# Where the matmul operands of a convolution and hard-swish kernel lie in SBUF: other offsets for w_in, y and y_other

## The chip, the cores and the metric

The kernel runs on one core of a Trainium2 chip. The time is the device time of one execution in microseconds (us), and the profile is one execution taken by the hardware profiler. Engines are named as in the profile: PE is TensorE's matmul, PEld its weight load, DVE is VectorE, ACT is ScalarE, POOL is GpSimd, SP is SyncE. SBUF is the on-chip memory of 128 partitions from which all of them read; an offset here is a byte address within a partition, the same in all partitions.

## What is computed

A depthwise causal convolution of 7 taps along the sequence, whose weights are a softmax per head, is followed by two dense layers with a hard-swish between them:

```
w   = exp(weight - max); w = w / (sum(w) + 1e-9)          # 8 heads x 7 taps
y   = sum over k of w[h, k] * x[b, s + k - 6, h, :]        # x: 8 x 4096 x 192
h   = y @ w_in                                            # 32768 x 192 @ 192 x 2048
g   = h * clip(h + 3, 0, 6) / 6
out = g @ w_out                                           # 2048 x 192
```

Everything is fp32 (the weights of the dense layers come as float64 words).

## The kernel before, in words

The 32768 tokens are worked on in 32 blocks of 1024. A block has two stages on TensorE.

First layer (`first_layer`, `products`, L443). A block of y is held as 128 partitions x 3 x 512: the lower 64 partitions have one half of the block's tokens, the upper 64 the other; the 192 channels are 64 partitions x 3. To keep fp32 accuracy with float32r matmuls, both operands are split: y into a high and a low part (`y_own`, tiles y0 and y1), w_in into a high, a low and a full part (`w_in_parts`, tiles w_in0, w_in1, w_in2). `PASSES` says which meet: (w_in0, y0), (w_in1, y0), (w_in2, y1). A unit of the first layer is 3 passes x 3 channel groups x 2 partition halves = 18 matmuls of 64x512, that is nine pairs; the two of a pair use the two halves of the array's rows, the lower for 128 hidden channels of its tokens, the upper for another 128 of its own. Each matmul has a weight load of 64x128. 8 units read `y_own`; 8 more read `y_other`, the same numbers with the partition halves exchanged by DMA, which gives each half of the tokens the hidden channels that it still lacks (`swap`, L304 and L305). So a block has 288 matmuls at L443 in 144 pairs. ACT (`relu`, L316) and DVE (`gate`, L320) make g from each unit's two PSUM banks.

Second layer (`second_layer`, L583). It is a two-level Strassen-like scheme over g, sums of g and sums of w_out. Four column groups of 32 run side by side, in an order that is written out by hand: each matmul has a due time in units of a 256-column matmul, and the list is sorted by these. Operands that move are g, the sums S1 and S3 (tiles s1 and s3), z, z_other and z_early; weights are w_out, w_s and w_s4. The sums S3 are made behind the gates of the first layer's second half by POOL (`g_sums`, L390) and, for the last chunks, by DVE; POOL makes the small sums too (`small_sums`, L541) and issues accumulating DMAs (L486, L775, L980). One of the second layer's streams begins with products of S3. The convolution of the block after the next (L966, L969) runs on ACT and DVE beside all this; `split_high`, `split_rest` and `swap_parts` then make the next block's operands.

The first block is different: before it the weights are rounded from float64 words, chunk by chunk, in `Rounding` (L192 to L232; L229, L230 and L231 write the three parts of w_in), between the units.

Tiles are placed in the order in which they are asked for, pool after pool (cst, xs, ys, yo, ot, and then the pools of the start or of the rest), each rounded up to 32 bytes. Worked out from the sizes, offsets before, relative to a multiple of 64:

| tiles | offset |
|---|---|
| g, w_in0, w_in1, w_in2, w_out, w_s, w_s4 | 32 |
| y0, y1 (also z_early), y_other (also z_other) | 32 |
| y (unsplit), results, s1, s3, z, p1, p4 | 0 |

Within these tiles all matmul operands start at multiples of 128 bytes.

Two tiles of the softmax are touched: `mx` (the maximum, in pool ot at L117) and `sm` (the sum, in pool yo at L126), one word each per partition; `e_sb` (the exponentials, L264) has a tile of its own. They are used at L263 to L268 and at L872 to L877, once, at the start.

Of the kernel before, what the change touches and what calls it, by code (L numbers as in the profile page):

```python
# [8 lines left out]
ALU = mybir.AluOpType  # L9
ACT = mybir.ActivationFunctionType  # L10
AX = mybir.AxisListType
F32 = mybir.dt.float32
# [19 lines left out]
def kernel(  # L32
# [8 lines left out]
    nc = tc.nc  # L41
    P = nc.NUM_PARTITIONS

    B, D, S = xT.shape
    H, KC = weight.shape
# [7 lines left out]
    K3 = D // D2  # L53
# [7 lines left out]
    NP = NC // 2  # L61
# [5 lines left out]
    cst = ctx.enter_context(tc.tile_pool(name="cst", bufs=1))  # L67
    xs = ctx.enter_context(tc.tile_pool(name="xs", bufs=1))
    ys = ctx.enter_context(tc.tile_pool(name="ys", bufs=1))
    yo = ctx.enter_context(tc.tile_pool(name="yo", bufs=1))  # L70
    ot = ctx.enter_context(tc.tile_pool(name="ot", bufs=1))
# [21 lines left out]
    w_sb = cst.tile([P, KC], F32, name="w_sb")  # L93
    for base, dma in ((0, nc.scalar), (D2, nc.sync)):
        dma.dma_start(
            out=w_sb[base : base + D2],
            in_=weight.unsqueeze(1).to_broadcast([H, GJ, KC]),
# [16 lines left out]
    make_identity(nc, ident[:])  # L114
    diag = cnv.tile([P, KC, P], F32, name="diag", bufs=1)
    g = cst.tile([P, NP, 2, G, N], F32, name="g")
    mx = ot.tile([P, 1], F32, name="mx")  # L117
    zeros = g[:, 0, 0, 0]
    nc.vector.memset(zeros, 0.0)


    w_in_parts = [cst.tile([P, NP, K3, P], F32, name=f"w_in{n}") for n in range(3)]
    def own_tiles(name):
        return [yo.tile([P, K3, N], F32, name=f"{name}{n}", tag=f"y{n}") for n in range(2)]

    sm = yo.tile([P, 1], F32, name="sm")  # L126
    y_own, z_early = own_tiles("y"), []

    def other_tile():
        return yo.tile([P, 2, K3, N], F32, name="y_other", tag="other")  # L130
# [127 lines left out]
    for n in range(5):  # L258
# [2 lines left out]
            load_x0(1, nc.sync, nc.sync)  # L261

    nc.vector.tensor_reduce(out=mx[:], in_=w_sb[:], axis=AX.X, op=ALU.max)  # L263
    e_sb = cst.tile([P, KC], F32, name="e_sb")  # L264
    nc.vector.tensor_tensor(
        out=e_sb[:], in0=w_sb[:], in1=mx[:].to_broadcast([P, KC]), op=ALU.subtract
    )
    nc.scalar.activation(e_sb[:], e_sb[:], ACT.Exp)  # L268

    c_sb = cst.tile([P, KC], F32, name="c_sb")  # L270
    half = cst.tile([P, 1], F32, name="half")
# [597 lines left out]
        units[n].part()  # L869

    with tc.manual_schedule():
        nc.vector.tensor_reduce(out=sm[:], in_=e_sb[:], axis=AX.X, op=ALU.add)  # L872
        nc.vector.tensor_scalar_add(sm[:], sm[:], 1e-9)
        nc.vector.reciprocal(sm[:], sm[:])
        nc.vector.tensor_tensor(
            out=c_sb[:], in0=e_sb[:], in1=sm[:].to_broadcast([P, KC]), op=ALU.mult
        )  # L877


# [12 lines left out]
        for _ in range(3):  # L892

            nc.tensor.matmul(  # L894
                out=psum[:, b], lhsT=zeros[:, 0:P], rhs=zeros, start=True, stop=True
# [92 lines left out]
        for r in range(2 * NP):  # L988
# [12 lines left out]
            n = joins.get(r)  # L1001
# [127 lines left out]
```

## Time and profile before

| | |
|---|---|
| median of 3 runs | 2198.15 us (2197.32 to 2198.38) |
| the profiled execution | 2197.43 us |
| its span, first to last instruction | 2195.7 us |
| granted TensorE clock | 0.999 |
| L443, first layer | 47% of the chain that ended last |
| L583, second layer | 49% |
| L443 matmuls, median ns of one | 386 |
| L443 weight loads, median ns | 184 |
| from one full block's start to the next | 67.47 us, of which the second layer 34.93 |
| first block | 17.3 to 94.7 us |

[...] The timeline of the profile gives the start of a group, its length, the engine, the line, what is written and read, and how many instructions are merged.

### The profile page before, as it was taken

What the parts mean: (1) busy time and instruction counts of PE and PEld (TensorE: products, weight loads), DVE (VectorE), ACT (ScalarE), POOL (GpSimd) and SP (SyncE); (2) the same over time, 40 slices, a digit from 0 to 9 for tenths busy, and PEclk for the clock granted to TensorE, in tenths of its full rate; (3) what the DMA queues carried; (4) which work ended last, traced back from release to release, by engine and by line L of the source; (5) the groups of instructions that cost most, each with busy time, mean ns of one, the idle gap of its engine ahead of it and who ended that gap; (6) DMA issues with size and microseconds to landing.
All of it is one profiled execution on the core that took longest, in us unless ns stands there. A gap on an engine that the chain in (4) does not pass through costs nothing.

```text
span 2195.7 us, 53684 instructions
## 1 busy us (share of the span) xinstructions
PE 2186.6 (100%) x23086; PEld 1568.1 (71%) x23086; DVE 1973.7 (90%) x1872; ACT 1267.6 (58%) x1761; POOL 1016.9 (46%) x864
## 2 busy tenths in 40 slices
PE   9999999999999999999999999999999999999998
PEld 5577776777777777777777767777777777677776
DVE  8889899899898998998988999989899998998987
ACT  7456565565655665555656556555566555565644
POOL 4545543355533555334554335553355533455433
PEclk9999999999999999999999999999999999999999
DMA  7366556756566665667555675656666566765564
GB/s 166 66 120 98 97 98 112 129 90 107 97 111 121 106 106 92 109 112 121 97 98 100 109 129 92 108 93 113 120 108 106 91 109 112 122 97 97 99 105 64
DMA packets 330557, 231.80 MB, mean 106 GB/s; under 512 B 209584, under 2 KB 294064, under 8 KB 330320
## 3 DMA queue, kind: packets, MB, share of 16 engines
q0 software_dynamic: 98688, 122.25, 36.5%
q1 hardware_dynamic: 230392, 105.86, 23.9%
q8 instruction: 181, 2.97, 0.6%
q14 instruction: 56, 0.46, 0.1%
q10 hardware_dynamic: 1240, 0.27, 0.1%
HBM read 31.72 MB, written 25.17 MB: 26 GB/s over the span
## 4 chain that ended last, share of the span: by engine, by line
PE 98%; DVE 1%; ACT 1%; POOL 0%; DMA 0%; issue 0%; DVEq 0%; ACTq 0%
PE psum L583 49%; PE psum L443 47%; PE psum L331 2%; PE psum L886 0%; PE psum L894 0%; DVE results L410 0%; ACT g L316 0%; DVE results L416 0%; DVE s L390 0%; DMA y_other<-y 0%; POOL w_in L231 0%; ACT scale L207 0%; ACT sig L204 0%; ACT sig L210 0%; POOL sig L221 0%
## 5 line engine op out<-in xcount | busy, mean ns | idle before, releaser
L583 PE MATMUL psum<-g,w_out 128*32 128x512 f32 (+1 forms) x5720 | 1024.7, 508 | 0.0
L583 PE MATMUL psum<-s,w_out 128*32 128x512 f32 (+1 forms) x3272 | 734.2, 570 | 0.0
L316 ACT ACTIVATE g<-psum,half 128x1024 f32<-128x1024 f32 x512 | 569.0, 1115 | 272.6 <-PE psum L443 270.4
L320 DVE SCALAR_TENSOR_TENSOR g<-g,psum 128x1024 f32<-128x1024 f32 x512 | 606.3, 1213 | 113.0 <-ACT g L316 112.7
L541 POOL TENSOR_TENSOR s<-g 128x256 f32<-128x256 f32 x248 | 272.0, 1097 | 759.5 <-DVE g L320 483.8
L583 PEld LDWEIGHTS psum<-g,w_out 128*32 128x32 f32 x5720 | 424.3, 110 | 169.9 <-issue 59.0
L443 PE MATMUL psum<-y,w_in 64*128 64x512 f32 x4608 | 535.0, 388 | 0.3 <-POOL w_in L231 0.2
L443 PE MATMUL psum<-y_other,w_in 64*128 64x512 f32 x4608 | 529.1, 386 | 0.0
L443 PEld LDWEIGHTS psum<-y,w_in 64*128 64x128 f32 x4608 | 431.6, 184 | 118.5 <-issue 26.0
L443 PEld LDWEIGHTS psum<-y_other,w_in 64*128 64x128 f32 x4608 | 435.0, 184 | 87.7 <-DMA y_other<-y 0.5
L583 PEld LDWEIGHTS psum<-s,w_out 128*32 128x32 f32 x3272 | 231.9, 110 | 107.4 <-issue 56.0
L969 DVE SCALAR_TENSOR_TENSOR y<-x,c_sb,y 128x1536 f32<-128x1536 f32 x156 | 291.9, 1871 | 1.9 <-ACT y L966 1.8
L583 PE MATMUL psum<-g,w_s 128*32 128x256 f32 x1488 | 289.4, 379 | 0.0
L390 POOL TENSOR_TENSOR s<-g 128x1024 f32<-128x1024 f32 x93 | 236.8, 2715 | 0.4 <-DVE g L320 0.4
L583 PE MATMUL psum<-z,w_s 128*32 128x256 f32 x992 | 235.1, 380 | 0.0
L390 DVE TENSOR_TENSOR s<-g 128x1024 f32<-128x1024 f32 x124 | 197.4, 1611 | 1.1
L483 ACT ACTIVATE z<-g 128x512 f32<-128x512 f32 x186 | 142.7, 767 | 63.0 <-DVE g L320 63.0
L583 PEld LDWEIGHTS psum<-g,w_s 128*32 128x32 f32 x1488 | 149.0, 110 | 32.1 <-DVE p L410 0.4
L583 PE MATMUL psum<-s,w_s 128*32 128x256 f32 x744 | 170.7, 379 | 0.0
L410 DVE TENSOR_TENSOR g<-g 128x1024 f32<-128x1024 f32 x124 | 143.6, 1220 | 1.1
L541 POOL TENSOR_TENSOR s<-g,s 128x256 f32<-128x256 f32 x124 | 143.6, 1158 | 0.0
L390 DVE TENSOR_TENSOR g<-g 128x2048 f32<-128x2048 f32 x62 | 139.4, 2286 | 1.0
(112 smaller groups left out, 2291.2 us busy)
## 6 DMA issues: line engine op xcount, KB each, us to landing
y_other<-y SPq DMA_DIRECT2D x124, 384.0 KB, 5.1
z<-g POOLq DMA_DIRECT2D x93, 512.0 KB, 5.6
z<-z POOLq DMA_DIRECT2D x62, 512.0 KB, 5.4
out_dram<-results SPq DMA_DIRECT2D x378, 64.0 KB, 2.6
y<-x POOLq DMA_DIRECT2D x30, 768.0 KB, 8.9
x<-in_x_dram SPq DMA_DIRECT2D x53, 388.5 KB, 7.1
g<-g POOLq DMA_DIRECT2D x31, 512.0 KB, 6.2
g<-in_moe_w_in_dram SPq DMA_DIRECT2D x16, 192.0 KB, 5.9
```

The lines of the kernel that those rows point to most:

```text
L316: nc.scalar.activation(r6, h, ACT.Relu, bias=half[:], scale=1.0 / 6.0)
L320: nc.vector.scalar_tensor_tensor(out=g_, in0=g_, scalar=1.0, in1=h, op0=ALU.min, op1=ALU.mult)
L331: lambda p=p: nc.tensor.matmul(out=bank[j * QS : (j + 1) * QS, tokens], lhsT=w_out[:, p, w, cols], rhs=x[:, p, tokens], start=(first and p ...
L390: engine.tensor_tensor(out=o[:, r], in0=a[:, r], in1=b[:, r], op=op)
L410: nc.vector.tensor_tensor(out=out, in0=x, in1=y, op=op)
L443: nc.tensor.matmul(out=psum[:, 2 * slot + k], lhsT=r32(w_in_parts[wn][r, c, s]), rhs=r32(y_other[0][r, yn, s] if group else y_own[yn][r, s ...
L483: nc.scalar.mul(to, x, sign)
L541: engine.tensor_tensor(out=o, in0=p, in1=q, op=op)
L583: nc.tensor.matmul(out=out, lhsT=w, rhs=x, start=start, stop=True, tile_position=(0, j * QS), skip_group_check=True,)
L969: nc.vector.scalar_tensor_tensor(out=y[:], in0=taps_of(k), scalar=c_sb[:, k : k + 1], in1=y[:], op0=ALU.mult, op1=ALU.add,)
```

## The change

The two unused ends of w_in1's and w_in2's tiles are new: 4 words ahead and 4 behind, and 2 ahead and 6 behind. `sm` becomes the eighth word of the tile of `e_sb`, which is now asked for ahead of w_out; `mx` goes between `y_own` and `y_other`. The instructions are the same in number, order and shape.

Offsets after, worked out in the same way: w_in0 as before (32 behind a multiple of 64), w_in1 at 48, w_in2 at 8; that is 0, 16 and 8 behind multiples of 32. y0 and y1 (and z_early) at 0; y_other (and z_other) at 32 as before. Everything that is placed behind w_in moves too: w_out, w_s, w_s4 to 0; results, s1, s3, z, p1, p4 to 32; the unsplit y stays at 0, and g at 32.

```diff
@@ -114,17 +114,26 @@
     make_identity(nc, ident[:])
     diag = cnv.tile([P, KC, P], F32, name="diag", bufs=1)
     g = cst.tile([P, NP, 2, G, N], F32, name="g")
-    mx = ot.tile([P, 1], F32, name="mx")
     zeros = g[:, 0, 0, 0]
     nc.vector.memset(zeros, 0.0)
 
 
-    w_in_parts = [cst.tile([P, NP, K3, P], F32, name=f"w_in{n}") for n in range(3)]
+
+    w_in_parts = []
+    for n, (ahead, behind) in enumerate(((0, 0), (4, 4), (2, 6))):
+        words = NP * K3 * P
+        whole = cst.tile([P, ahead + words + behind], F32, name=f"w_in{n}")
+        w_in_parts.append(
+            whole[:, ahead : ahead + words].rearrange("p (j s f) -> p j s f", s=K3, f=P)
+        )
+
     def own_tiles(name):
         return [yo.tile([P, K3, N], F32, name=f"{name}{n}", tag=f"y{n}") for n in range(2)]
 
-    sm = yo.tile([P, 1], F32, name="sm")
+    e_tile = cst.tile([P, KC + 1], F32, name="e_sb")
+    sm = e_tile[:, KC : KC + 1]
     y_own, z_early = own_tiles("y"), []
+    mx = yo.tile([P, 1], F32, name="mx")
 
     def other_tile():
         return yo.tile([P, 2, K3, N], F32, name="y_other", tag="other")
@@ -261,11 +270,11 @@
             load_x0(1, nc.sync, nc.sync)
 
     nc.vector.tensor_reduce(out=mx[:], in_=w_sb[:], axis=AX.X, op=ALU.max)
-    e_sb = cst.tile([P, KC], F32, name="e_sb")
+    e_sb = e_tile[:, :KC]
     nc.vector.tensor_tensor(
-        out=e_sb[:], in0=w_sb[:], in1=mx[:].to_broadcast([P, KC]), op=ALU.subtract
+        out=e_sb, in0=w_sb[:], in1=mx[:].to_broadcast([P, KC]), op=ALU.subtract
     )
-    nc.scalar.activation(e_sb[:], e_sb[:], ACT.Exp)
+    nc.scalar.activation(e_sb, e_sb, ACT.Exp)
 
     c_sb = cst.tile([P, KC], F32, name="c_sb")
     half = cst.tile([P, 1], F32, name="half")
@@ -869,11 +878,11 @@
         units[n].part()
 
     with tc.manual_schedule():
-        nc.vector.tensor_reduce(out=sm[:], in_=e_sb[:], axis=AX.X, op=ALU.add)
-        nc.vector.tensor_scalar_add(sm[:], sm[:], 1e-9)
-        nc.vector.reciprocal(sm[:], sm[:])
+        nc.vector.tensor_reduce(out=sm, in_=e_sb, axis=AX.X, op=ALU.add)
+        nc.vector.tensor_scalar_add(sm, sm, 1e-9)
+        nc.vector.reciprocal(sm, sm)
         nc.vector.tensor_tensor(
-            out=c_sb[:], in0=e_sb[:], in1=sm[:].to_broadcast([P, KC]), op=ALU.mult
+            out=c_sb[:], in0=e_sb, in1=sm.to_broadcast([P, KC]), op=ALU.mult
         )
 
 
```

## The prediction

> **What bounds the kernel now.** First the page's busy times and its chain of work that ended last, to find the engine and lines that carry the end:
>
> ```profile
> PE 2186.6 (100%) x23086; PEld 1568.1 (71%) x23086; DVE 1973.7 (90%) x1872; ACT 1267.6 (58%) x1761; POOL 1016.9 (46%) x864
> PE 98%; DVE 1%; ACT 1%; POOL 0%; DMA 0%; issue 0%; DVEq 0%; ACTq 0%
> ```
>
> TensorE is the whole chain: 49% of it L583, 47% L443. A faster kernel needs matmuls that start closer together; nothing beside TensorE can give time, but it can take it. So the next view is the timeline of one block's matmuls: the first layer (L443), then the start of the second (L583).
>
> ```profile
> 1039.60 16.61 PE L443 MATMUL psum<-y,w_in 64*128 64x512 f32 x144
> 1056.05 16.48 PE L443 MATMUL psum<-y_other,w_in 64*128 64x512 f32 x144
> 1072.46 0.40 PE L583 MATMUL psum<-g,w_out 128*32 128x256 f32 x1
> ...
> 1072.71 0.38 PE L583 MATMUL psum<-z,w_s 128*32 128x256 f32 x1
> ...
> 1072.92 0.38 PE L583 MATMUL psum<-z,w_s 128*32 128x256 f32 x1
> ...
> 1073.14 0.38 PE L583 MATMUL psum<-z,w_s 128*32 128x256 f32 x1
> ...
> 1073.36 0.38 PE L583 MATMUL psum<-z,w_s 128*32 128x256 f32 x1
> ```
>
> The matmuls of L443 go in pairs (two halves of the partitions), 72 pairs for y and 72 for y_other. Starts are 16.45 and 16.41 us apart: 228 ns a pair with the hand-over; single starts in the trace are 226 or 227 ns apart in 4322 of 4522 back-to-back steps, a settled 226.67. The 256-column fp32 matmuls of L583 follow each other at (1073.36 - 1072.71) / 3 = 216.7 ns. So a pair has some 10 ns above a neighbour of nearly the same duration (379 against 386 ns below). That is all there is to win at this line.
>
> Third, the durations, by tile and in the stretch just after a block's first matmul has waited:
>
> ```profile
> L443 PE MATMUL psum<-y,w_in x4608: 383/386/501, 17.3 to 2137.1; 64*128 64x512 f32 x192
> L443 PE MATMUL psum<-y_other,w_in x4608: 385/386/498, 18.7 to 2153.5; 64*128 64x512 f32 x192
> L443 PE MATMUL psum<-y,w_in x12: 386/391/496, 94.7 to 95.9; 64*128 64x512 f32 x12
> ```
>
> The columns are least/median/most ns. At fixed addresses the same matmul takes 386 ns once settled, but a median of 391 in the first pairs, whose starts are 236, 228, 233 and 231 ns apart before 226.67 holds. What differs there is only the moment at which weight load and stream meet (the load starts 2.5 instead of 3.3 ns behind the matmul, by the average of 26 block starts). Something in how they meet costs 383 to 398 ns; addresses may be a second way to move it.
>
> Last, POOL, because L583 begins with sums that POOL makes:
>
> ```profile
> 1067.32 2.41 POOL L390 TENSOR_TENSOR s<-g 128x1024 f32<-128x1024 f32 x1
> 1069.68 1.26 POOL L486 DMA_DIRECT2D z<-z  x1
> 1070.48 5.23 POOL L390 TENSOR_TENSOR s<-g 128x1024 f32<-128x1024 f32 x2
> PEld psum L583 <- POOL s L390: 0.4, 2, 0.2
> ```
>
> POOL works without a gap and ends its last sum at 1075.71, 3.25 us after the second layer's first matmul. Over the 30 full blocks that end lies 2.3 to 3.6 us behind. In six blocks it is 3.55 to 3.60, and there the second layer is 0.20 to 0.22 us longer than the 34.93 us of the rest. So the limit is about 3.38 us, and the median block (3.22) is 0.16 us away from it.
>
> **The change part by part.** (1) The softmax's small tiles. The same reductions, subtraction, exponential and reciprocal on the same 128x1 and 128x7 shapes, in the same order on DVE and ACT; none added. sm reads and shares the tile of e_sb, and both writers are in an order that they already had. Cost 0, covered by the 17 us before the first L443 matmul.
>
> (2) Writing w_in at its new offsets: 8 each of ACT L229 (512 ns), POOL L230 (545) and L231 (1086). If off-32 writes were a tenth slower it would be 8 x 0.21 = 1.7 us, all in the first block, where TensorE waited for L231 0.2 us in all. Taken 0, ends 0 and +1.7.
>
> (3) Everything behind w_in moves. w_out, w_s, w_s4 and z_early come to multiples of 64; results, S1, S3, z, p1, p4 leave them by 32. In L583 today g and z_other lie 32 off and s and z on a multiple: s against g is 592 and 592 ns, z_other, z and s at 256 columns 379, 379 and 379. No difference in 1 ns, so 0; were it 1 ns for each of 160 steps in 31 blocks, 5 us either way. The swap DMAs land in 5.1 us; TensorE waited for them 0.5 us in the whole run: 0.
>
> (4) What L443 reads. Before, the three parts of w_in, both y's and y_other are all 32 bytes off a multiple of 64. After: w_in0 stays; w_in1 is 16 bytes, w_in2 8 bytes further off a multiple of 32; y_own is on a multiple of 64, y_other stays. So of the six pairings of stationary and moving operand only w_in0 with y_other is as it was. No run here shows another alignment, so it is bounded. Best: L583's 216.7, -10.0 ns a pair. Worst: the unsettled steps' mean, (236 + 228 + 233 + 231) / 4 = 232.0, +5.3 ns. Between them the nearest row of the same matmul is its least duration, 383 against 386: -3.0 ns. I take this: the offsets no longer move all six reads in step, and the trace shows that the same instruction can do 383. The first block is paced by the rounding of the weights (94.7 us to its end against 67.5 for others) and counts nothing. That leaves 31 x 144 = 4464 pairs x 3.0 = 13.4 us, 0.43 us a block.
>
> (5) What is late next. The second layer starts 0.43 us earlier in each block while POOL, full from its first L541 on, ends when it did. Adding 0.43 to each block's distance and counting what exceeds 3.38 (less what exceeds it now) gives 6.4 us in 22 of the 30 blocks: behind the waiting S3 matmul all of TensorE's queue stands. Taken 6.4; if POOL's sums came forward with the gates, 0.
>
> Sum against the profiled execution's own 2197.43 us (span 2195.7 and 1.7 around it): -13.4 + 6.4 = -7.0, 2190.4. The median of the runs is 0.7 above the profiled one: 2191.
>
> **The rivals.** *Out of step (slower).* The settled 226.67 is already near the shortest that L443 shows, and it is one rhythm that every unit repeats because all reads lie alike. With parts at 0, 16 and 8 the meeting of load and stream changes at each pass, three times in nine pairs, and the pairs never settle. For it: each restart takes four to five pairs to settle, and 390 to 398 are as regular there as 386. Against it: loads begun 72 and 154 ns late still had 226 to 227 ns steps. Price: 4464 x 5.3 = 23.7 us, less 1.3 for POOL's six waits that vanish: 2220.5. It decides once the mean step is above 226.67; at two thirds of the pairs (w_in1, w_in2) it is 15.8, 2213.
>
> *Nothing happens.* The matmul before a pause, with no weight load beside it, takes 385 against 386, so reading weights costs the stream 1 ns at most, and the rest of the 10 ns might be the form of this matmul. Price 0: 2198. [...]
>
> *The whole 10 ns go.* 4464 x 10.0 = 44.6 us, 1.44 a block; POOL's waits then take back 35.4 by the same count, 2188.9. Only if POOL's chain came forward too would it be 2153.
>
> **How the numbers follow.** Forecast 0.41, whole 10 ns 0.07, nothing (or a gain too small to tell) 0.12, out of step 0.40. A measurement of this kernel tells 0.2% (4.4 us) from no change: faster 0.48, same 0.12, slower 0.40. The range takes in the slower case whole, to 2222, and below reaches to 2176, part of the way to a POOL that follows; the forecast alone would be 2186 to 2195.
>
> **What would show it.** L443's two halves of a block: 16.45 and 16.41 us now; right if near 16.2, and POOL's L390 end then 3.5 to 3.7 us behind L583's start with "PEld psum L583 <- POOL s L390" or longer second layers (35.1 and more instead of 34.93). The y half should change more than the y_other half, since there all three pairings are new. Wrong if the median duration of L443 is 390 or more (out of step), if it stays 386 in both rows (nothing), or if L583's 592 or 379 move, which I cost at 0.

## The result, and the profile after

The changed kernel takes 2219.48 us (median of 4 runs, 2219.35 to 2219.82) against 2197.98 us of the kernel before (4 runs, 2197.32 to 2198.38): 1.0098 times, with a 95% interval of 1.0081 to 1.0116. It is slower by 21.5 us, and the granted clock is 0.999 in both. The forecast was 2191, and its range reached to 2222.

The page of the changed kernel (busy times; the chain of work that ended last by engine, then the first entries by line are the two matmul lines, now L592 and L452 at 48% each):

```profile
PE 2208.6 (100%) x23086; PEld 1576.8 (71%) x23086; DVE 1966.5 (89%) x1872; ACT 1270.0 (57%) x1761; POOL 1020.4 (46%) x864
PE 98%; DVE 1%; DMA 0%; ACT 0%; SPq 0%; issue 0%; POOL 0%; DVEq 0%; ACTq 0%
```

TensorE still is the whole chain. All line numbers behind the edit are nine higher: L443 is now L452, L583 is L592, L390 is L399. The timeline of the same block's matmuls after the change (start us, length us, engine, line, tiles, shape, count):

```profile
1050.10 16.99 PE L452 MATMUL psum<-y,w_in 64*128 64x512 f32 x144
1066.93 16.86 PE L452 MATMUL psum<-y_other,w_in 64*128 64x512 f32 x144
1083.72 0.40 PE L592 MATMUL psum<-g,w_out 128*32 128x256 f32 x1
```

The starts are 16.83 and 16.79 us apart where they were 16.45 and 16.41. By tile (least/median/most ns):

```profile
L452 PE MATMUL psum<-y,w_in x4608: 384/392/502, 16.8 to 2158.7; 64*128 64x512 f32 x192
L452 PE MATMUL psum<-y_other,w_in x4608: 383/391/497, 18.3 to 2175.4; 64*128 64x512 f32 x192
```

The least duration is what it was (383 or 384); the median went from 386 to 392 and 391. The matmuls of the second layer kept theirs (line, tiles, shape, count, then busy us and mean ns):

```profile
L592 PE MATMUL psum<-g,w_out 128*32 128x512 f32 x3456 | 870.6, 592 | 0.0
L592 PE MATMUL psum<-s,w_out 128*32 128x512 f32 x2928 | 728.3, 592 | 0.0
...
L592 PE MATMUL psum<-z,w_s 128*32 128x256 f32 x992 | 235.1, 380 | 0.0
L592 PE MATMUL psum<-s,w_s 128*32 128x256 f32 x744 | 170.7, 379 | 0.0
L592 PE MATMUL psum<-z_other,w_out 128*32 128x256 f32 x744 | 118.0, 379 | 0.0
```

Worked out from single starts in the two traces, without the first block: the mean step, which is the distance from one pair's start to the next, went from 227.06 to 232.22 ns in the y half and from 226.67 to 231.90 ns in the y_other half. Without the first six pairs of each y half, which hadn't settled before either, the y half goes from 226.77 to 232.51. A first layer, from its first pair's start to its last pair's, takes 33.30 us instead of 32.57; 31 of them give 22.8 us. A second layer, from there to the next block's first pair, takes 34.94 instead of a mean of 34.97, which gives back 1.0 us in 30 of them; the first block is 0.1 longer. The sum is 21.9 us, the difference of the two spans (2217.6 and 2195.7).

The steps no longer settle. In block 10 of the kernel before, the steps are 226 or 227 ns from the sixth pair to the end. After the change, units of the y half repeat 235, 233, 232, 238, 232, 230, 228, 234, 231 ns, and units of the y_other half 237, 232, 236, 233, 229, 228, 231, 232, 229 ns, unit after unit.

### The profile page after: what moved, and what is told of

Its sections match the earlier page's. It is cut to its first block, busy times and chain, and to the rows that moved or that the text cites. A ratio compares the mean times of both kernels' runs of the same rounds, so it can differ in the third digit from the quotient of the medians.

```text
span 2217.6 us, 53684 instructions
## 1 busy us (share of the span) xinstructions
PE 2208.6 (100%) x23086; PEld 1576.8 (71%) x23086; DVE 1966.5 (89%) x1872; ACT 1270.0 (57%) x1761; POOL 1020.4 (46%) x864
## 4 chain that ended last, share of the span: by engine, by line
PE 98%; DVE 1%; DMA 0%; ACT 0%; SPq 0%; issue 0%; POOL 0%; DVEq 0%; ACTq 0%
PE psum L592 48%; PE psum L452 48%; PE psum L340 2%; PE psum L895 0%; DMA stage<-in_moe_w_out_dram 0%; PE psum L903 0%; DVE results L419 0%; DVE results L425 0%; DMA y_other<-y 0%; DVE s L399 0%; ACT g L325 0%; DVE scale L201 0%; SPq L163 0%; POOL w_in L240 0%; ACT sig L219 0%
## 5 line engine op out<-in xcount | busy, mean ns | idle before, releaser
L592 PE MATMUL psum<-g,w_out 128*32 128x512 f32 (+1 forms) x5720 | 1023.5, 508 | 0.0
L592 PE MATMUL psum<-s,w_out 128*32 128x512 f32 (+1 forms) x3272 | 735.4, 570 | 0.0
L550 POOL TENSOR_TENSOR s<-g 128x256 f32<-128x256 f32 x248 | 261.9, 1056 | 760.3 <-DVE g L329 508.8
L452 PE MATMUL psum<-y,w_in 64*128 64x512 f32 x4608 | 546.6, 393 | 0.2
L592 PEld LDWEIGHTS psum<-g,w_out 128*32 128x32 f32 x5720 | 422.0, 110 | 171.4 <-issue 62.1
L452 PE MATMUL psum<-y_other,w_in 64*128 64x512 f32 x4608 | 541.3, 391 | 0.1
L452 PEld LDWEIGHTS psum<-y,w_in 64*128 64x128 f32 x4608 | 433.1, 185 | 128.2 <-issue 26.0
L452 PEld LDWEIGHTS psum<-y_other,w_in 64*128 64x128 f32 x4608 | 436.3, 184 | 98.4 <-DMA y_other<-y 0.5
L592 PEld LDWEIGHTS psum<-s,w_out 128*32 128x32 f32 x3272 | 228.2, 110 | 103.3 <-issue 53.8
L592 PE MATMUL psum<-g,w_s 128*32 128x256 f32 x1488 | 289.3, 379 | 0.0
L399 POOL TENSOR_TENSOR s<-g 128x1024 f32<-128x1024 f32 x93 | 236.8, 2715 | 0.7 <-DVE g L329 0.7
L592 PE MATMUL psum<-z,w_s 128*32 128x256 f32 x992 | 235.1, 380 | 0.0
L399 DVE TENSOR_TENSOR s<-g 128x1024 f32<-128x1024 f32 x124 | 185.1, 1512 | 1.1
L592 PEld LDWEIGHTS psum<-g,w_s 128*32 128x32 f32 x1488 | 149.8, 110 | 31.9
L592 PE MATMUL psum<-s,w_s 128*32 128x256 f32 x744 | 170.7, 379 | 0.0
L419 DVE TENSOR_TENSOR results<-psum,results 32x256 f32<-32x256 f32 (+2 forms) x221 | 107.8, 488 | 39.4 <-PE psum L592 34.2
```

Source lines behind the costliest of these rows:

```text
L399: engine.tensor_tensor(out=o[:, r], in0=a[:, r], in1=b[:, r], op=op)
L419: nc.vector.tensor_tensor(out=out, in0=x, in1=y, op=op)
L452: nc.tensor.matmul(out=psum[:, 2 * slot + k], lhsT=r32(w_in_parts[wn][r, c, s]), rhs=r32(y_other[0][r, yn, s] if group else y_own[yn][r, s ...
L550: engine.tensor_tensor(out=o, in0=p, in1=q, op=op)
L592: nc.tensor.matmul(out=out, lhsT=w, rhs=x, start=start, stop=True, tile_position=(0, j * QS), skip_group_check=True,)
```

## The experiments

The theory after the result was the rival of the prediction, "out of step": unequal offsets of successive weight loads keep the pairs from settling. The competing theories: the position of y against the weights decides, or a weight load that starts off a multiple of 32 bytes costs by itself, or the operands behind w_in that moved too. Offsets below are given behind multiples of 128 bytes, because the runs turned out to need that. Before: w_in0, w_in1, w_in2, y0, y1, y_other all at 32. After: w_in at 32, 48 and 72, y0 and y1 at 64, y_other at 96. "y/y_other" steps are means of a pair's step in ns in the two halves of the first layer, in the y half without its first six pairs. The first four runs, the four scans and y_plus64 were executed once each, undo_wy ten times, w_alone and y_alone four times.

### The first four: which part

`w_only` moves y's own parts, in the changed kernel:

```diff
+    mx = yo.tile([P, 1], F32, name="mx")
     y_own, z_early = own_tiles("y"), []
-    mx = yo.tile([P, 1], F32, name="mx")
```

> w_in0, w_in1, w_in2 at 0, 16 and 8 bytes behind multiples of 32 as in the changed kernel, y's own parts back at 32 off a multiple of 64 beside y_other. Out of step (unequal offsets of successive weight loads keep the pairs from settling): both halves of the first layer stay unsettled, means of 231 to 233 ns a pair in both, about 2219 us. If y's own position is what costs: the y half falls back to 226.7 ns and the time to 2207 to 2209 us.

Measured: 2217.0 us, steps 231.4/231.6. Both halves stay unsettled. But y and y_other lie at 96 here, not at 32 as before, so it leaves open whether the weights alone do it.

`y_only` gives the weights equal offsets behind multiples of 64 in the changed kernel:

```diff
-    for n, (ahead, behind) in enumerate(((0, 0), (4, 4), (2, 6))):
+    for n, (ahead, behind) in enumerate(((0, 0), (0, 8), (8, 0))):
```

> All three parts of w_in at one offset (32 off a multiple of 64, as before the change), y's own parts on a multiple of 64, y_other 32 off. Out of step: equal weight offsets settle again, 226.7 ns a pair in both halves, 2198 us within 2. If the position of the moving operand against the weights costs: the y half stays at 232 ns a pair, the y_other half at 226.7, 2209 us. It also tests everything placed behind w_in (second layer): 34.93 us if that is free.

Measured: 2211.9 us, 232.5/228.3. The y half doesn't settle with weights that lie alike within 64 bytes; but w_in2 is 64 further on, at 96, so "out of step" in its narrow form falls only with all8 and y_alone below, where the weights lie alike within 128 and the pairs don't settle either. The y_other half doesn't reach the 226.7 that the competing theory expected of it. The second layers take 34.93 us.

`all16` and `all8` put the three parts in one tile, 4 or 2 words behind its start (y at 64 and y_other at 96 as in the changed kernel):

```diff
+    words = NP * K3 * P
+    whole = cst.tile([P, 4 + 3 * words + 12], F32, name="w_in")
+    w_in_parts = [
+        whole[:, 4 + n * words : 4 + (n + 1) * words].rearrange("p (j s f) -> p j s f", s=K3, f=P)
+        for n in range(3)
+    ]
```

> All three parts of w_in 16 bytes behind a multiple of 32, y and y_other as in the changed kernel. Out of step: the offset itself is free and only unequal offsets cost, so 226.7 ns a pair in both halves, 2198 us within 2. If a weight load that starts off a multiple of 32 costs by itself: 230 ns a pair or more in every position of the unit, 2215 us or more.

> All three parts of w_in 8 bytes behind a multiple of 32. Out of step: 226.7 ns a pair in both halves, 2198 us within 2. [...]

Measured: all16 2210.1 us, 227.4/231.9; all8 2215.9 us, 231.1/230.7. Neither theory holds. At 16 bytes the y half ends at 226.67 in 17 of the 31 blocks, in some from the seventh pair on, so an offset off 32 need not cost; the y_other half, with the same weights, doesn't settle. In the other 14 blocks the y half ends in a cycle of four pairs (229, 229, 229 and 226 ns, a mean of 228.3), at the same places. Two neighbouring blocks by their durations (least/median/most ns), the first of the one kind and the second of the other:

```profile
L451 PE MATMUL psum<-y,w_in x144: 386/386/499, 1113.9 to 1130.1; 64*128 64x512 f32 x144
L451 PE MATMUL psum<-y,w_in x144: 384/388/498, 1181.8 to 1198.1; 64*128 64x512 f32 x144
```

So the same places can end in more than one rhythm. At 8 bytes the y half runs evenly too, but at 231. How the two positions go together seems to matter, and the scans test that.

### Four scans: y's place against the weights'

The own parts of y get one tile with room to move, and each block takes another place in it; the weights keep one offset in a run. So each run gives the step at 25 or 31 places of y in the y halves of its blocks, in the kernel before (the softmax's small tiles share their neighbours' padding to make the room, and y_other comes to 96):

```diff
+    offsets = list(range(31))
+
     def own_tiles(name):
-        return [yo.tile([P, K3, N], F32, name=f"{name}{n}", tag=f"y{n}") for n in range(2)]
+        at = offsets.pop(0) if name == "y" else 0
+        whole = yo.tile([P, 32 + 2 * K3 * N], F32, name=name, tag="own")
+        return [
+            whole[:, at + n * K3 * N : at + (n + 1) * K3 * N].rearrange("p (s t) -> p s t", t=N)
+            for n in range(2)
+        ]
```

In `scan_y` the weights are at 32; in `scan_y_w8`, `scan_y_w4` and `scan_y_w12` they are at 40, 36 and 44 (2, 1 and 3 words ahead in one tile, as in all8), with y from 0 to 96.

> All parts of w_in 32 behind a multiple of 128; y's own pair of tiles moves by 4 bytes from block to block, from 96 behind a multiple of 128 through 0 to 88; y_other fixed at 96. The steps of each block's y half give the cost of that one relative position. If only unequal offsets cost (out of step as forecast): 226.7 ns in every block. If the relative position of stream and weights decides: 226.7 at y = 32 (same position as the weights) and at y = 48 (16 behind, as with all parts at 16), 231 at y = 56, 232 near y = 0, smooth or stepped between. If y's absolute position decides, it can't be told from this run alone.

> The same with all parts of w_in 8 bytes further on (40 behind a multiple of 128); y from 0 to 96 in steps of 4 bytes, y_other at 96. Relative position: the pattern of the first scan is found again, moved by 8 bytes (226.7 at y = 40 and 56). y's own position: the same pattern unmoved (226.7 at 32 and 48). The weights' own position: 231 ns throughout.

> The scan with all parts of w_in 36 behind a multiple of 128. If y's place within 16 bytes sets the class and the weights only the finer steps: again 235 to 240 at y = 4 + 16k and 229 to 232 at 12 + 16k. If it is the weights' place within 16 bytes against y's: the bad places move by 4 bytes to 8 + 16k. A step below 226.7 anywhere would point to a kernel faster than both.

> The scan with all parts of w_in 44 behind a multiple of 128. y's place alone: bad places stay at 4 + 16k. Relative place: they move by 12 bytes to 0 + 16k. A step below 226.7 anywhere would point to a kernel faster than both.

Four neighbouring blocks of scan_y by the durations of their y half (least/median/most ns), y at 32, 36, 40 and 44 with the weights at 32:

```profile
L450 PE MATMUL psum<-y,w_in x144: 383/386/493, 1186.7 to 1203.0; 64*128 64x512 f32 x144
L450 PE MATMUL psum<-y,w_in x144: 391/398/490, 1254.4 to 1271.4; 64*128 64x512 f32 x144
L450 PE MATMUL psum<-y,w_in x144: 387/392/493, 1322.9 to 1339.5; 64*128 64x512 f32 x144
L450 PE MATMUL psum<-y,w_in x144: 386/388/497, 1391.3 to 1407.7; 64*128 64x512 f32 x144
```

Their steps are 226.7, 238.6, 233.3 and 229.7 ns: four bytes make 12 ns. Two places of scan_y_w8, y at 68 and 76 with the weights at 40, have the same order:

```profile
L455 PE MATMUL psum<-y,w_in x144: 391/396/499, 1254.3 to 1271.3; 64*128 64x512 f32 x144
...
L455 PE MATMUL psum<-y,w_in x144: 386/387/489, 1391.1 to 1407.4; 64*128 64x512 f32 x144
```

All y halves together (for each block the median of its units' mean steps, then the mean over the blocks with that place, in brackets least and most):

| y's place within 16 bytes | weights at 32 | at 36 | at 40 | at 44 |
|---|---|---|---|---|
| 0 | 232.9 (226.7 to 236.4) | 232.5 (226.7 to 234.7) | 231.7 (230.4 to 233.2) | 231.4 (227.4 to 235.1) |
| 4 | 238.7 (235.6 to 240.0) | 239.0 (237.6 to 240.0) | 237.6 (234.8 to 240.0) | 237.4 (233.9 to 240.0) |
| 8 | 233.7 (232.6 to 237.0) | 234.4 (232.6 to 235.6) | 233.6 (231.1 to 237.0) | 233.8 (230.8 to 236.2) |
| 12 | 230.2 (229.3 to 231.9) | 230.3 (229.2 to 231.1) | 230.5 (229.2 to 231.9) | 231.0 (229.7 to 233.3) |

The four runs took 2218.6, 2226.6, 2219.4 and 2229.0 us in the order of the columns. The rows don't move when the weights move: it is y's own place within 16 bytes that orders the means, and the expected shift by 8, 4 or 12 bytes is not there. The blocks at 4 (233.9 and more) and at 12 (233.3 and less) don't overlap; those at 0 and 8 overlap with both. In the last three runs six places come twice: 16 of these 18 repeats agree within 0.2 ns, the other two within 2.3. Within the row of 0, where y lies in both kernels, the step still ranges from 226.7 to 236.4 with the weights fixed at 32, by y's place within 128. The settled 226.7 comes at y 32 with weights at 32 (the kernel before), at y 48 with weights at 36, and not at y 48 with weights at 32 (232.0), where it was expected. No half of any block in these four runs has a mean step below 226.67, so no faster kernel came out of them.

The weights' place counts as well. y_other lies at 96 in all four runs, and in most blocks it ran at 228.9, 233.2, 230.7 and 235 ns with the weights at 32, 36, 40 and 44. But position doesn't decide alone: with weights at 32 y_other ran at 233.3 in five blocks, with weights at 44 at 226.7 in two, at the same addresses. The place of the half that ran before it differs between these blocks, but that this is the reason is not shown; in all16 nothing was moved between blocks, and two rhythms came all the same. The steps are cycles that the pairs fall into, and a pair of positions can have more than one.

### The rest of the change, and 64 bytes

`undo_wy` is the changed kernel with the operands of the first layer back at 32, and all that lies behind them still moved; `y_plus64` moves both y's on by 64 from there:

```diff
-    for n, (ahead, behind) in enumerate(((0, 0), (4, 4), (2, 6))):
+    for n, (ahead, behind) in enumerate(((0, 0), (0, 0), (0, 0))):
...
+    mx = yo.tile([P, 1], F32, name="mx")
     y_own, z_early = own_tiles("y"), []
-    mx = yo.tile([P, 1], F32, name="mx")
```

(in y_plus64 the tile of mx has 24 words).

> The changed kernel with w_in's parts and both y's back at 32 behind a multiple of 128; all that lies behind w_in stays moved (w_out and its sums on a multiple of 64, results, S1, S3, z 32 off). If the first layer's operands are the whole cause: 226.7 ns in both halves, 34.93 us a second layer, same as before within 0.1%. If the moved operands of the second layer cost too: slower by what the second layers show.

> The same, but y's own parts and y_other both 64 bytes further on (96 behind a multiple of 128, weights at 32). If the pattern repeats every 64 bytes: 226.7 ns in both halves, 2198 us. If 64 bytes count: about 233 ns in the y half and 229 in the y_other half as in the block of the first scan that had both at 96, 2216 to 2218 us.

Measured: undo_wy 2197.95 us, 1.0002 times the kernel before (0.9992 to 1.0011). The first layer of one block by the timeline, then the durations of undo_wy, and then those of y_plus64:

```profile
1039.99 16.61 PE L452 MATMUL psum<-y,w_in 64*128 64x512 f32 x144
1056.44 16.48 PE L452 MATMUL psum<-y_other,w_in 64*128 64x512 f32 x144
```

```profile
L452 PE MATMUL psum<-y,w_in x4608: 383/386/501, 17.0 to 2137.9; 64*128 64x512 f32 x192
L452 PE MATMUL psum<-y_other,w_in x4608: 385/386/498, 18.5 to 2154.2; 64*128 64x512 f32 x192
```

```profile
L452 PE MATMUL psum<-y,w_in x4608: 384/389/503, 17.2 to 2145.4; 64*128 64x512 f32 x192
L452 PE MATMUL psum<-y_other,w_in x4608: 384/388/492, 18.7 to 2161.9; 64*128 64x512 f32 x192
```

The 16.45 us between the two starts of undo_wy are back, steps are 226.8/226.7, and the second layers take 34.93 us in the median. So w_out, its sums, results, S1, S3, z and the moved small tiles cost nothing: the whole loss lies in the operands of the first layer. In this run w_out and what follows it lie 64 bytes from their places in the changed kernel, but there the second layers of 34.94 us show no cost either. y_plus64 took 2205.9 us with steps of 228.9/228.9 in a cycle of three (226, 229 and 232 ns), less than the 2216 expected from the y half of the scan, but clearly not settled: the pattern doesn't repeat every 64 bytes. That half of the scan had the same places within 128 bytes and a cycle of two (231 and 236 ns, a mean of 233.4). Its y lay 128 bytes away from y_plus64's, so whether the distance or a second rhythm makes this difference stays open.

### Each part alone, with the other where it was

`w_alone` has the weights at 32, 48 and 72 and both y's at 32. Against the changed kernel, mx and half go into the padding of w_sb and c_sb, and the two tiles that are saved bring y and y_other back to 32:

```diff
-    w_sb = cst.tile([P, KC], F32, name="w_sb")
+    w_tile = cst.tile([P, KC + 1], F32, name="w_sb")
+    w_sb, mx = w_tile[:, :KC], w_tile[:, KC : KC + 1]
...
-    mx = yo.tile([P, 1], F32, name="mx")
...
-    c_sb = cst.tile([P, KC], F32, name="c_sb")
-    half = cst.tile([P, 1], F32, name="half")
+    c_tile = cst.tile([P, KC + 1], F32, name="c_sb")
+    c_sb, half = c_tile[:, :KC], c_tile[:, KC : KC + 1]
```

`y_alone` has the weights at 32 and y at 64, y_other at 96:

```diff
-    for n, (ahead, behind) in enumerate(((0, 0), (4, 4), (2, 6))):
+    for n, (ahead, behind) in enumerate(((0, 0), (0, 0), (0, 0))):
...
+    mx = yo.tile([P, 16], F32, name="mx")[:, 0:1]
     y_own, z_early = own_tiles("y"), []
-    mx = yo.tile([P, 1], F32, name="mx")
+    yo.tile([P, 8], F32, name="gap")
```

> Only w_in's three parts as in the changed kernel (32, 48 and 72 behind a multiple of 128); y's own parts and y_other at 32 as before the change. If either operand's move is enough to lose the settled step: 230 to 233 ns a pair in both halves, 2213 to 2219 us. If the losses of the two moves add up: less than the changed kernel by what y alone costs, so about 2204 to 2208 us.

> Only the y's as in the changed kernel (own parts at 64, y_other at 96 behind a multiple of 128); w_in at 32 as before. From the scan: about 233 ns a pair in the y half, 229 in the y_other half, 2211 to 2214 us; then the two moves together (2219.5) cost less than the sum of each alone. If they add up: below 2210 us.

Measured: w_alone 2220.2 us, 1.0101 times before (1.0084 to 1.0118), steps 232.6/232.6. y_alone 2215.3 us, 1.0081 times (1.0066 to 1.0096), steps 233.3/229.0. The block beginning at 1051 us in w_alone, and then that at 1048 in y_alone:

```profile
L452 PE MATMUL psum<-y,w_in x144: 388/391/496, 1051.2 to 1067.8; 64*128 64x512 f32 x144
L452 PE MATMUL psum<-y_other,w_in x144: 388/391/396, 1068.1 to 1084.6; 64*128 64x512 f32 x144
```

```profile
L453 PE MATMUL psum<-y,w_in x144: 389/392/495, 1048.3 to 1065.0; 64*128 64x512 f32 x144
L453 PE MATMUL psum<-y_other,w_in x144: 384/388/396, 1065.2 to 1081.5; 64*128 64x512 f32 x144
```

Alone the parts cost 22.3 and 17.5 us; together 21.5. Both times are about 1 us above the ranges expected for this case, and far from those for losses that add up. They don't add up: either one is enough to lose the settled step. The weights are written only in the first block (the last write of w_alone starts at 62.4 us), so in the later blocks of w_alone nothing but the place from which the weights are read has changed for the first layer's matmuls.

## Why the prediction was wrong, point by point

**What bounds the kernel** held: the chain is TensorE, and the time went where L443's pairs start.

**Steps 1 to 3** (small tiles, writing w_in, everything behind w_in) were taken at 0. For the small tiles and for what lies behind w_in undo_wy shows 0 within 0.1%. It has w_in at its old places, so step 2 is read from the changed kernel: its three writes take a median of 514, 547 and 1042 ns (512, 545 and 1086 before), and the first block is 0.1 us longer. The durations of the second layer are the same to 1 ns, as the rows of s and g had said.

**Step 4 is the one that failed.** It took 3.0 ns off each pair, and 5.2 ns more were measured in each half. The place where it went wrong is the choice between the bounds. I took the least duration of the row, 383, as the nearest row, and a difference of durations for one of steps. These aren't the same: a matmul of 386 ns lasts beyond the next pair's start, 226.67 ns on, so the time goes by the starts. In the kernel before, eight of the 4608 matmuls with y take 383, all of them among pairs that hadn't settled, next to others of 390 to 394; after the change the least is still 384 and 383, beside medians of 392 and 391. The reason given (the offsets no longer move all six reads in step) turned out the other way: that they lay alike went with the short step, and moving either operand lost it. The stretch of unsettled pairs, median 391, which I had put down as the worst case, had the right sign, and its +5.3 ns is close to what came. That it is so close is luck in part, since other places gave anything from 0 to 13 ns above 226.7.

**The rival "out of step"** had the place and the price (2220.5 forecast, 2219.5 measured; 5.3 ns, and 5.2 measured), and 0.40 of the chance. The sign that the prediction named for it, a median of 390 or more, came. Its reason was too narrow: it blamed the unequal offsets of the three parts. y_alone and all8 lose the settled step with equal ones. What the runs show is that the step of 226.67 is an exception, which the arrangement before (weights and y's all at 32 behind a multiple of 128) has in both halves, and that moving either operand as the change does loses it (232.6 in both halves of w_alone, 233.3 and 229.0 in y_alone). Elsewhere it came at few places: in one block of scan_y_w4, in part of the blocks of all16 and in two halves of scan_y_w12.

**The rival "nothing happens"** is out. It rested on the matmul without a weight load beside it taking 385 against 386, which was a comparison inside the settled arrangement. That the place of the weights is free, w_alone doesn't bear out: with y untouched it made the steps 5.8 and 5.9 ns longer.

**Step 5** was sized for a faster first layer, which didn't come, so its 6.4 us weren't tested. Its other end was: in the changed kernel POOL's last sum ends 1.7 to 3.1 us behind the second layer's start (2.3 to 3.6 before), and the six second layers that were longer (by 0.17 to 0.22 us; the prediction's 0.20 is too high for one of them) are gone. Counted from the second layer's first matmul to the next block's first pair, that gave back the 1.3 us that the rival took for it; of these 1.0 are left, because in each block the step from the first layer to the second became 0.01 us longer.

**The forecast on the halves** ("the y half should change more") didn't come true: the mean step rose by 5.2 ns in both. Only without the first six pairs does the y half change more, 5.7 ns. Its reason fails too: w_alone changes both halves by nearly the same, 5.8 and 5.9.

**The chances.** 0.48 for faster came from treating an unexplored arrangement as if it could go either way. The profile said more than that: the settled step of 226.67 ns was the shortest regular one of L443, and nearly everything beside it was longer (228 to 236 ns in the pairs ahead of it).

## What to carry to other kernels

Where a matmul stream repeats one exact step thousands of times, look at its steps before it settles: here they had the sign and nearly the size of what another placement cost (5.3 ns above the settled step; 5.2 measured), and the least value in a row did not (3.0 below). This is one case, and no rule. Placement of operands is worth 1% here (1.0098 times) and can be lost by an edit that shifts a tile by a few bytes, a small tile put ahead of y included (from undo_wy to y_plus64 only the size of such a tile changes: 2197.95 and 2205.93 us), so the offsets of both matmul operands belong in the comparison whenever a layout changes. A scan that moves one operand from block to block in a single run gives 30 positions for the price of one.

## What the runs showed of the hardware that was not expected

- The step of a 64x512 float32r pair went, in its mean over many places, with the moving operand's place within 16 bytes: means of 237 to 239 ns at 4, 233 to 234 at 8, 231 to 233 at 0 and 230 to 231 at 12, at four places of the weights. No run shows why 4 is the slowest and 12 the fastest in the mean.
- The weights' place moves the step as well: y_other at 96 has 228.9, 233.2, 230.7 and 235 ns in most blocks, with the weights at 32, 36, 40 and 44.
- 64 bytes matter too: the arrangement before with both y's 64 bytes further on has 228.9 instead of 226.7 ns.
- Steps fall into cycles of one, two, three, four or nine pairs, and the same addresses can have several: y_other at 96 with the weights at 44 ran at 235 or at 226.7 ns, and the y half of all16 at 226.7 or at 228.3.
- The fp32 matmuls of the second layer, of which four run side by side, show none of this: 592 and 379 ns at the offsets of both kernels, all multiples of 32.

Open stays what inside TensorE or its reads makes the cycles: that both operands' places matter is shown; why they do is not, and no run here tells whether weight load and stream get in each other's way. It also stays open whether an arrangement below 226.67 ns exists; none of the tried ones had it.
